# Last 64 keys of two head pairs: float32 64x64 products behind the product with v, in place of split half-row products

## The chip, the cores and the metric

One core of one Trainium2 chip runs the whole program. The metric is the device time of one execution in microseconds (us), the median of several runs.

## The reference

The program is an attention layer with sigmoid weights, followed by a mixture of eight experts. `q`, `k` and `v` have the shape (8 batches, 12 heads, 448 tokens, 64), in float32.

```python
scores = scale * np.matmul(q, k.transpose(0, 1, 3, 2)) - np.log(S)   # scale = 1/8, S = 448
attn = 1.0 / (1.0 + np.exp(-scores))
x = np.matmul(attn, v).astype(np.float32)      # then (B*S, H*D) = (3584, 768)
logits = x @ w_gate                            # 8 experts, 448 tokens each at most
# all (token, expert) pairs in falling order of logit; a pair is taken
# if its token is still free and its expert not full
out[mask_e] = np.maximum(x[mask_e] @ w1[e], 0.0) @ w2[e]
```

The weights are `w1` (8, 768, 1024) and `w2` (8, 1024, 768). The choice of experts hangs on the order of the logits, so the attention is computed to float32 accuracy.

## The kernel before

**Three parts.** The attention runs first, over 48 pairs of heads (8 batches of 6 pairs). Then the router finds each expert's tokens. Then the experts' two matrix products run, with the routing of later experts between them.

**A pair.** The two heads of a pair lie on the two halves of the 128 partitions: head j has partitions 64j to 64j+63, which are its 64 dimensions (`LO` and `HI` in the code). `load` brings k and q of a pair, and v of two pairs. `turn` (L394) transposes k and q of a pair on VectorE into `kqT` (L398), then `split` writes a high part `kqH` in float32r on ScalarE (L404) and the rest `kqL` on VectorE (L405). Keys times queries are then three products, high by high, high by low and low by high (`products`, L414 to L416). Each is one matrix instruction for each of the two heads, on rows 0 to 63 and on rows 64 to 127 of the array.

**Chunks of keys.** The 448 keys of a pair are three chunks of 128 and a rest of 64. `scores(b, pr, c)` computes chunk c for both heads into a tile `sc` of PSUM, of which there are three, and ScalarE's sigmoid (L428) writes the tile `at`. The rests of two neighbouring pairs, an even one and the odd one behind it, share one tile: `c == 3`, run with the odd pair. It first computes the last 128 keys of the even pair into all 128 rows, and then the last 64 keys of the odd pair over rows 0 to 63. What stays in rows 64 to 127 are the last 64 keys of the even pair.

**Product with v.** `av` (L441) multiplies the three full chunks by v, in plain float32. A float32 product in source is two matrix instructions in the trace. The two heads use the two halves of the array's columns. For an odd pair, four more float32 products take the rests of both pairs (L447). Each of them uses 64 rows and 64 columns of the array, and they go to two tiles `tp` of PSUM, of which there are two in all. VectorE then copies (L449) and adds (L451) into `xt`.

**Order.** The order in each engine is that of the program. Iteration i of the loop over pairs does: loads (on even pairs), `turn` of pair i+1, chunk 0 of the scores of pair i, `split` of pair i+1, the other chunks of pair i, up to two pieces of background work, and then `av` of pair i-1. Background work is the gate's logits of a finished batch (L462, added into `LE` at L464) and, for the first batch, the transposes of its rows (L473) with copies on VectorE (L478). Those of the other batches come after the loop, with copies on ScalarE (L476). Tiles `kqT`, `kqH` and `kqL` have two buffers each, which pairs take in turn.

Of the kernel before, what the change touches and what calls it, by code (L numbers as in the profile page):

```python
# [7 lines left out]
F32 = mybir.dt.float32  # L8
# [5 lines left out]
AF = mybir.ActivationFunctionType  # L14
# [11 lines left out]
AT_BUFS = 8  # L26
# [16 lines left out]
def _s32(v):  # L43
    v &= 0xFFFFFFFF
    return v - (1 << 32) if v >= (1 << 31) else v
# [65 lines left out]
class Router:  # L111
# [42 lines left out]
    def search(self, pe):  # L154
# [7 lines left out]
        nc.vector.tensor_copy(KE, p[:, :224])  # L162
        T, JP = K.c0, None
        X = None if pe else self.bank().bitcast(I32)
        for st in range(16):
            sh = 30 - 2 * st
            cnt = wk.tile([128, 3], BF, name="r_cnt") if pe else K.CN
            for i in range(3):
                junk = wk.tile([128, 224], BF, name="r_junk")
                nc.vector.tensor_scalar(junk, KE, T[:, i:i + 1].bitcast(F32), None, OP.is_ge, OP.add,  # L170
                                        accum_out=cnt[:, i:i + 1])
# [24 lines left out]
            if st == 0:  # L196
# [4 lines left out]
                nc.vector.tensor_scalar(nJ, PF, _s32(0x80000000), J, OP.bitwise_or, OP.bitwise_xor)  # L201
                T = wk.tile([128, 3], I32, name="r_T")
                nc.vector.tensor_scalar(T, K.kk[:, 1], nJ, None, OP.bitwise_xor)
            else:
                if st < 15:
                    T = wk.tile([128, 3], I32, name="r_T")
                    nc.vector.scalar_tensor_tensor(T, acc.bitcast(I32).to_broadcast([128, 3]), sh, nX,
                                                   OP.logical_shift_left, OP.bitwise_xor)
# [123 lines left out]
def moe_attention(tc, q, k, v, w_gate, w1, w2, out):  # L332
    nc = tc.nc
    B, H, S, D = q.shape
# [5 lines left out]
    with contextlib.ExitStack() as ctx:  # L340
# [7 lines left out]
        ps_s = pctx.enter_context(tc.tile_pool(name="pa_s", bufs=3, space=PSUM))  # L348
        ld = actx.enter_context(tc.tile_pool(name="ld", bufs=2))
        wk = actx.enter_context(tc.tile_pool(name="wk", bufs=2))  # L350
# [5 lines left out]
        bias = cp.tile([128, 1], F32, name="bias")  # L356
# [4 lines left out]
        LO, HI = slice(0, 64), slice(64, 128)  # L361
        def load(b, g, qq=nc.gpsimd, vq=nc.sync):


            nat["v", b, g] = ld.tile([128, G4, 3, D], F32, name="nv", bufs=3)
            nat["r", b, g] = ld.tile([128, 2, D], F32, name="nr", bufs=3)
            for i in range(2):
                t = nat["kq", b, 2 * g + i] = ld.tile([128, 2, S // 32, 32], F32, name="nkq", bufs=4)
                for n, (qn, src) in enumerate(((nc.sync, k), (qq, q))):
                    for j in range(2):  # L370
                        rws = src[b, g * G4 + 2 * i + j].rearrange("(c p) (x d) -> x p c d", p=32, x=2)
                        for x in range(2):
                            o = 64 * j + 32 * x
                            qn.dma_start(t[o:o + 32, n], rws[x])  # L374
            vs = v[b, g * G4:(g + 1) * G4]
            for h in range(G4):
                vq.dma_start(nat["v", b, g][:, h], vs[h, :384].rearrange("(c p) d -> p c d", p=128))
            for i in range(2):
                vq.dma_start(nat["r", b, g][HI if i == 0 else LO],
                             vs[2 * i:2 * i + 2, 384:].rearrange("h p d -> p h d"))  # L380
# [9 lines left out]
        for s in range(4):  # L390
            nc.sync.dma_start(wgz[:, :, s, 8 * s:8 * s + 8], w_gate.rearrange("(c p) e -> p c e", p=128))

        KQ = {}
        def turn(b, pr):  # L394


            T = wk.tile([128, 2, S], F32, name="kqT")
            nc.vector.transpose(T.rearrange("p n t -> p (n t)"), nat["kq", b, pr].rearrange("p n c d -> p (n c d)"))  # L398
            H = wk.tile([128, 2, S], F32R, name="kqH")
            L = wk.tile([128, 2, S], F32R, name="kqL")  # L400
            KQ[b, pr] = [x[:, i] for i in range(2) for x in (H, L)]

            def split():
                nc.scalar.activation(H, T, AF.Copy)  # L404
                nc.vector.tensor_tensor(L, T, H.bitcast(F32), OP.subtract)  # L405
            return split

        AT = {}

        def products(p, b, pr, keys, m):  # L410


            KH, KL, QH, QL = KQ[b, pr]
            for i, (R, M) in enumerate(((KH, QH), (KH, QL), (KL, QH))):  # L414
                for j, half in enumerate((LO, HI)):
                    nc.tensor.matmul(p[:m, j, :S], R[half, keys], M[half], start=i == 0, stop=i == 2)  # L416

        def scores(b, pr, c):


            a = AT[b, pr, c] = wk.tile([128, 2, S], F32, name="at", bufs=AT_BUFS)
            p = ps_s.tile([128, 2, 512], F32, name="sc")
            if c < 3:
                products(p, b, pr, slice(c * 128, c * 128 + 128), 128)
            else:
                products(p, b, pr - 1, slice(S - 128, S), 128)
                products(p, b, pr, slice(S - 64, S), 64)
            nc.scalar.activation(a, p[:, :, :S], AF.Sigmoid, bias=bias, scale=1 / math.sqrt(D))  # L428

        XT = {}  # L430

        def av(b, pr):


            if pr == 0:
                XT[b] = xa.tile([128, NP, S], F32, name="xt", bufs=XT_BUFS)
            p = ps_t.tile([128, 512], F32, name="tp")
            g, h0 = (2 * pr) // G4, (2 * pr) % G4
            for c in range(3):
                for j in range(2):  # L440
                    nc.tensor.matmul(p[j * 64:j * 64 + 64, :S], nat["v", b, g][:, h0 + j, c, :],  # L441
                                     AT[b, pr, c][:, j, :], start=(c == 0), stop=(c == 2 and pr % 2 == 0))
            if pr % 2:
                r = ps_t.tile([128, 512], F32, name="tp")
                for j in range(2):
                    for half, o in ((HI, r), (LO, p)):
                        nc.tensor.matmul(o[j * 64:j * 64 + 64, :S], nat["r", b, g][half, j, :],  # L447
                                         AT[b, pr, 3][half, j, :], start=o is r, stop=True)
            nc.vector.tensor_copy(XT[b][:, pr, :], p[:, :S])  # L449
            if pr % 2:  # L450
                nc.vector.tensor_tensor(XT[b][:, pr - 1, :], r[:, :S], XT[b][:, pr - 1, :], OP.add)  # L451
# [4 lines left out]
        def logits(b, prs):  # L456

            s, g = b % 4, b // 4
            p = ps_t.tile([128, 512], F32, name="tp")
            for pr in prs:  # L460
                for c in range(NCH):
                    nc.tensor.matmul(p[32 * c:32 * c + 32, :CP], wgz[:, pr, s, :], XT[b][:, pr, c * CP:(c + 1) * CP],  # L462
                                     start=(pr == prs[0]), stop=(pr == prs[-1]))
            nc.vector.tensor_tensor(LE[:, g], LE[:, g], p[:, :CP], OP.add)  # L464
# [17 lines left out]
        pairs = [(b, pr) for b in range(B) for pr in range(NP)]  # L482
        NPR = len(pairs)
        turn(*pairs[0])()
        bg, late = [], []
        for i in range(NPR + 1):
            cur = pairs[i] if i < NPR else None
            nxt = pairs[i + 1] if i + 1 < NPR else None
            old = pairs[i - 1] if i else None
            if cur and cur[1] % 2 == 0:  # L490
                nx = i // 2 + 2
                if nx < NPR // 2:
                    load(nx // 3, nx % 3)
            split = turn(*nxt) if nxt else None
            for c in range(4 if cur and cur[1] % 2 else 3 if cur else 0):
                scores(*cur, c)
                if c == 0 and split:
                    split()
            for _ in range(2):
                if bg:  # L500
                    bg.pop(0)()
            if old:
                av(*old)
            if i == 2:
                route_consts(nc, cp, K)
            if old == (B - 1, NP - 2):
                bg.append(lambda: logits(B - 1, range(NP - 2)))
            if old and old[1] == NP - 1:
                b = old[0]
                if b < B - 1:  # L510
                    bg.append(lambda b=b: logits(b, range(NP)))
                for c in range(NCH):
                    for hf in range(2):
                        if b >= B - LATE:
                            late.append(lambda b=b, c=c, hf=hf: rows(b, c, hf, "act"))
                        else:
                            bg.append(lambda b=b, c=c, hf=hf: rows(b, c, hf, "dve"))
# [8 lines left out]
        ps_s = ctx.enter_context(tc.tile_pool(name="ps_s", bufs=2, space=PSUM))  # L526
        ps_a = ctx.enter_context(tc.tile_pool(name="ps_a", bufs=2, space=PSUM))
        R = Router(tc, K, cp, rw, ps_a)
# [208 lines left out]
        for kx in range(E):  # L737
            turned = kx + 1 == E
            start = clock[0]
# [16 lines left out]
            for step, cost in enumerate(moe(kx)):  # L756
# [9 lines left out]
                if t >= t_chore:  # L766
                    c = next((c for c in chores if c[0] <= t), None)
# [37 lines left out]
```

## Time and profile before

| what | before |
|---|---|
| median of 3 runs | 913.71 us (912.76 to 914.37) |
| profiled execution | 915.77 us, its span 914.0 us |
| TensorE matrix instructions | 860.7 us busy, 94% of the span |
| VectorE | 535.1 us, 59% |
| ScalarE | 457.7 us, 50% |
| GpSimd | 463.7 us, 51% |
| attention | from 0 to about 303 us of the span |
| router alone, with the late rows | about 303 to 356 us |
| experts | about 356 to 914 us |

All times of rows below are from the one profiled execution, in us from the start of its span. A row of the timeline has the start, the duration from the first start to the last end, the engine, the line, the operation, the tile written and the tiles read, the part of the array (rows\*columns), the shape that is streamed, the count, and in brackets the idle time of the engine before it and what ended it. PE is TensorE's matrix engine and PEld its loading of the stationary operand; DVE is VectorE, ACT is ScalarE. The end of a matrix instruction is modelled, and neighbours overlap, so distances between starts tell more than durations.

### The profile page before, as it was taken

What the parts mean: (1) busy time and instruction counts of PE and PEld (TensorE: products, weight loads), DVE (VectorE), ACT (ScalarE), POOL (GpSimd) and SP (SyncE); (2) the same over time, 40 slices, a digit from 0 to 9 for tenths busy, and PEclk for the clock granted to TensorE, in tenths of its full rate; (3) what the DMA queues carried; (4) which work ended last, traced back from release to release, by engine and by line L of the source; (5) the groups of instructions that cost most, each with busy time, mean ns of one, the idle gap of its engine ahead of it and who ended that gap; (6) DMA issues with size and microseconds to landing.
All of it is one profiled execution on the core that took longest, in us unless ns stands there. A gap on an engine that the chain in (4) does not pass through costs nothing.

```text
span 914.0 us, 16457 instructions
## 1 busy us (share of the span) xinstructions
PE 860.7 (94%) x5603; PEld 656.2 (72%) x5603; DVE 535.1 (59%) x2053; ACT 457.7 (50%) x633; POOL 463.7 (51%) x442
## 2 busy tenths in 40 slices
PE   5898999999999774998999999999999999999997
PEld 3444555555555444987998888988988888989996
DVE  3645455555554588876968969959779632330110
ACT  5565676676677472443433534534434434544441
POOL 8533444444430003573675675684784783741651
PEclk9999999999999996999899999999999999999999
DMA  9646665555550486324434343353452442632421
GB/s 176 140 97 149 126 128 117 116 125 118 116 121 1 127 277 185 108 82 149 140 114 146 122 147 124 128 151 113 154 162 96 141 154 90 213 117 82 158 76 61
DMA packets 205236, 117.59 MB, mean 129 GB/s; under 512 B 145728, under 2 KB 194880, under 8 KB 205152
## 3 DMA queue, kind: packets, MB, share of 16 engines
q1 hardware_dynamic: 190688, 83.03, 35.2%
q0 software_dynamic: 10752, 33.05, 11.4%
q10 hardware_dynamic: 3712, 0.46, 0.3%
q8 instruction: 44, 0.72, 0.3%
q14 instruction: 40, 0.33, 0.1%
HBM read 94.47 MB, written 22.02 MB: 127 GB/s over the span
## 4 chain that ended last, share of the span: by engine, by line
PE 78%; DVE 11%; issue 4%; DMA 2%; POOL 2%; ACT 2%; SPq 0%; POOLq 0%; ACTq 0%; DVEq 0%
PE sc L416 14%; PE tp L441 12%; PE sc L671 9%; PE sc L669 9%; PE sc L673 9%; PE sc L706 6%; PE sc L708 6%; PE sc L704 6%; DVE r_junk L170 3%; PE tp L447 2%; PE tp L634 2%; PE tp L621 2%; DMA xr<-xs,r_idx 1%; PE tp L462 1%; POOL wl L587 1%
## 5 line engine op out<-in xcount | busy, mean ns | idle before, releaser
L587 POOL TENSOR_TENSOR wl<-wr,wh 128x768 fp32r<-128x768 f32 (+1 forms) x96 | 205.7, 2151 | 135.5 <-ACT wh L585 124.6
L428 ACT ACTIVATE at<-sc,bias 128x896 f32<-128x896 f32 x168 | 160.6, 1003 | 63.2 <-PE sc L416 62.9
L374 POOL DMA_DIRECT2D nkq<-in_q_dram x184 | 115.5, 640 | 142.3 <-DVE kqT L398 132.9
L708 PE MATMUL sc<-hh,wl 128*128 128x448 f32 (+2 forms) x400 | 151.4, 379 | 0.0
L673 PE MATMUL sc<-xh,wl 128*128 128x448 f32 (+2 forms) x396 | 146.7, 370 | 0.0
L671 PE MATMUL sc<-xl,wh 128*128 128x448 f32 (+2 forms) x396 | 146.3, 370 | 0.0
L706 PE MATMUL sc<-hl,wh 128*128 128x448 f32 (+2 forms) x400 | 145.5, 364 | 0.2 <-POOL hl L681 0.2
L669 PE MATMUL sc<-xh,wh 128*128 128x448 f32 (+2 forms) x396 | 145.4, 367 | 0.0
L704 PE MATMUL sc<-hh,wh 128*128 128x448 f32 (+2 forms) x400 | 143.9, 360 | 0.0
L170 DVE TENSOR_SCALAR_CACHE_REDUCE r_junk<-r_KE,r_T 128x224 bf16<-128x224 f32 x315 | 123.3, 442 | 0.1
L441 PE MATMUL tp<-at,nv 128*64 128x448 f32 x576 | 118.8, 548 | 4.8 <-DVE xr L478 4.4
L585 ACT ACTIVATE wh<-wr 128x768 fp32r<-128x768 f32 (+1 forms) x112 | 102.0, 939 | 9.7 <-DMA wr<-in_moe_w_dram 9.7
L405 DVE TENSOR_TENSOR kqL<-kqT,kqH 128x896 fp32r<-128x896 f32 x48 | 52.4, 1092 | 68.5 <-ACT kqH L404 68.5
L681 POOL TENSOR_TENSOR hl<-yt,hh 128x896 fp32r<-128x896 f32 x32 | 68.2, 2132 | 46.7 <-ACT yt L680 45.1
L416 PE MATMUL sc<-kqH 64*128 64x448 f32 (+1 forms) x384 | 79.3, 410 | 11.7 <-ACT kqH L404 8.8
L677 ACT ACTIVATE hh<-sc 128x896 fp32r<-128x896 f32 x32 | 29.4, 919 | 111.5 <-PE sc L673 111.5
L441 PEld LDWEIGHTS tp<-at,nv 128*64 128x64 f32 x576 | 37.0, 136 | 63.7 <-issue 55.3
L706 PEld LDWEIGHTS sc<-hl,wh 128*128 128x128 f32 x400 | 75.2, 188 | 7.3 <-issue 1.1
L671 PEld LDWEIGHTS sc<-xl,wh 128*128 128x128 f32 x396 | 75.5, 191 | 6.5 <-issue 0.4
L669 PEld LDWEIGHTS sc<-xh,wh 128*128 128x128 f32 x396 | 75.7, 191 | 5.7
L607 POOL DMA_INDIRECT xr<-xs,r_idx x32 | 31.9, 997 | 94.0 <-ACT wh L585 83.2
L673 PEld LDWEIGHTS sc<-xh,wl 128*128 128x128 f32 x396 | 75.5, 191 | 5.0
(155 smaller groups left out, 1327.3 us busy)
## 6 DMA issues: line engine op xcount, KB each, us to landing
wr<-in_moe_w_dram SPq DMA_DIRECT2D x64, 384.0 KB, 3.0
wr<-in_moe_w_dram SPq DMA_DIRECT2D x48, 512.0 KB, 3.9
nkq<-in_k_dram SPq DMA_DIRECT2D x192, 56.0 KB, 2.5
xs<-xr SPq DMA_DIRECT2D x32, 336.0 KB, 3.3
nkq<-in_q_dram POOLq DMA_DIRECT2D x184, 56.0 KB, 2.6
nv<-in_v_dram SPq DMA_DIRECT2D x92, 96.0 KB, 2.4
nr<-in_v_dram SPq DMA_DIRECT2D x46, 32.0 KB, 2.3
xr<-xs,r_idx POOLq DMA_INDIRECT x32, 4.6
```

What stands on the lines that cost most here:

```text
L170: nc.vector.tensor_scalar(junk, KE, T[:, i:i + 1].bitcast(F32), None, OP.is_ge, OP.add, accum_out=cnt[:, i:i + 1])
L374: qn.dma_start(t[o:o + 32, n], rws[x])
L416: nc.tensor.matmul(p[:m, j, :S], R[half, keys], M[half], start=i == 0, stop=i == 2)
L428: nc.scalar.activation(a, p[:, :, :S], AF.Sigmoid, bias=bias, scale=1 / math.sqrt(D))
L441: nc.tensor.matmul(p[j * 64:j * 64 + 64, :S], nat["v", b, g][:, h0 + j, c, :], AT[b, pr, c][:, j, :], start=(c == 0), stop=(c == 2 and pr ...
L587: eng.tensor_tensor(lo, raw[u], hi.bitcast(F32), OP.subtract)
L669: nc.tensor.matmul(ph[:, f, lo:hi], wh[:, a, fs], xh[:, dd, lo:hi], start=st, stop=False)
L671: nc.tensor.matmul(ph[:, f, lo:hi], wh[:, a, fs], xl[:, dd, lo:hi], start=False, stop=False)
L673: nc.tensor.matmul(ph[:, f, lo:hi], wl[:, a, fs], xh[:, dd, lo:hi], start=False, stop=en)
L704: nc.tensor.matmul(py[:, d2, :w], wh[:, a, dsl], h1, start=st, stop=False)
L706: nc.tensor.matmul(py[:, d2, :w], wh[:, a, dsl], h2, start=False, stop=False)
L708: nc.tensor.matmul(py[:, d2, :w], wl[:, a, dsl], h1, start=False, stop=(j == 1 and a == 3))
```

## The change

The rest's scores are no longer made of split operands, and no longer with the odd pair's chunks. A new `rest_scores` makes them from `kqT` itself, in float32: for each of the two pairs and each of the two heads one product of the last 64 keys, on 64 rows and 64 columns of the array. The even pair's keys go to rows 64 to 127 of the tile, the odd pair's to rows 0 to 63, as before. It is called on iterations of even pairs, right behind `av` of the odd pair before, for the current (even) and the next (odd) pair. `kqT` gets three buffers, since it is now read by the matrix engine an iteration later. `scores` does three chunks for every pair; `products` is folded into it.

```diff
-            T = wk.tile([128, 2, S], F32, name="kqT")
+            T = KT[b, pr] = wk.tile([128, 2, S], F32, name="kqT", bufs=3)
...
         def scores(b, pr, c):
             a = AT[b, pr, c] = wk.tile([128, 2, S], F32, name="at", bufs=AT_BUFS)
             p = ps_s.tile([128, 2, 512], F32, name="sc")
-            if c < 3:
-                products(p, b, pr, slice(c * 128, c * 128 + 128), 128)
-            else:
-                products(p, b, pr - 1, slice(S - 128, S), 128)
-                products(p, b, pr, slice(S - 64, S), 64)
-            nc.scalar.activation(a, p[:, :, :S], AF.Sigmoid, bias=bias, scale=1 / math.sqrt(D))
+            KH, KL, QH, QL = KQ[b, pr]
+            for i, (R, M) in enumerate(((KH, QH), (KH, QL), (KL, QH))):
+                for j, half in enumerate((LO, HI)):
+                    nc.tensor.matmul(p[:, j, :S], R[half, c * 128:(c + 1) * 128], M[half], start=i == 0, stop=i == 2)
+            sigmoid(a, p)
+
+        def rest_scores(b, pr):
+            a = AT[b, pr, 3] = wk.tile([128, 2, S], F32, name="at", bufs=AT_BUFS)
+            p = ps_s.tile([128, 2, 512], F32, name="sc")
+            for o, T in ((HI, KT[b, pr - 1]), (LO, KT[b, pr])):
+                for j, half in enumerate((LO, HI)):
+                    nc.tensor.matmul(p[o, j, :S], T[half, 0, S - 64:S], T[half, 1], start=True, stop=True)
+            sigmoid(a, p)
...
-            for c in range(4 if cur and cur[1] % 2 else 3 if cur else 0):
+            for c in range(3 if cur else 0):
                 scores(*cur, c)
...
             if old:
                 av(*old)
+            if cur and cur[1] % 2 == 0:
+                rest_scores(*nxt)
```

## Rows read from the trace of the kernel before

**Rows 1.** The page: busy time by engine, and the chain's shares by engine.

```profile
PE 860.7 (94%) x5603; PEld 656.2 (72%) x5603; DVE 535.1 (59%) x2053; ACT 457.7 (50%) x633; POOL 463.7 (51%) x442
...
PE 78%; DVE 11%; issue 4%; DMA 2%; POOL 2%; ACT 2%; SPq 0%; POOLq 0%; ACTq 0%; DVEq 0%
```

**Rows 2.** Busy time in stretches: length, engines (instructions), granted clock, DMA share, GB/s.

```profile
107.83:242.00 134.17, 134.17 (x1120) 72.17 (x1116) 70.11 (x85) 96.09 (x104) 57.64 (x92) 1.00 0.60 122
...
303.00:345.00 42.00, 29.70 (x213) 18.76 (x205) 34.79 (x196) 25.71 (x56) 0.00 (x0) 1.00 0.72 231
```

**Rows 3.** Waits of the matrix engine, 0 to 300 us: total, times, longest.

```profile
PE sc L416 <- ACT kqH L404: 8.8, 1, 8.8
PE tp L441 <- DVE xr L478: 4.4, 3, 1.6
PE sc L416 <- ACT at L428: 2.9, 1, 2.9
```

**Rows 4.** Timeline of the matrix engine, one even and one odd pair.

```profile
241.98 0.47 PE L416 MATMUL sc<-kqH 64*128 64x448 f32 x2
...
243.70 0.37 PE L416 MATMUL sc<-kqH,kqL 64*128 64x448 f32 x2
244.00 2.48 PE L441 MATMUL tp<-at,nv 128*64 128x448 f32 x12
246.40 0.98 PE L447 MATMUL tp<-at,nr 64*64 64x448 f32 x8
247.32 0.47 PE L416 MATMUL sc<-kqH 64*128 64x448 f32 x2
...
249.06 0.37 PE L416 MATMUL sc<-kqH,kqL 64*128 64x448 f32 x2
249.36 0.47 PE L416 MATMUL sc<-kqH 64*128 64x448 f32 x2
...
249.87 0.37 PE L416 MATMUL sc<-kqH,kqL 64*128 64x448 f32 x2
250.07 0.36 PE L416 MATMUL sc<-kqH 64*64 64x448 f32 x2
...
250.77 2.48 PE L441 MATMUL tp<-at,nv 128*64 128x448 f32 x12
253.17 0.47 PE L416 MATMUL sc<-kqH 64*128 64x448 f32 x2
```

**Rows 5.** Timeline, matrix engine alone, 247.02 to 247.3: second half of L447's eight.

```profile
246.83 0.56 PE L447 MATMUL tp<-at,nr 64*64 64x448 f32 x4
```

**Rows 6.** Timeline of the weight loads within one product with v.

```profile
244.43 0.14 PEld L441 LDWEIGHTS tp<-at,nv 128*64 128x64 f32 x2 [0.23 <-issue]
244.80 0.14 PEld L441 LDWEIGHTS tp<-at,nv 128*64 128x64 f32 x2 [0.23 <-issue]
```

**Rows 7.** One line's instructions: duration min/median/max, first and last start, forms.

```profile
L447 PE MATMUL tp<-at,nr x192: 536/562/587, 24.2 to 303.0; 64*64 64x448 f32 x192
```

**Rows 8.** Timeline of ScalarE, the odd pair of rows 4.

```profile
248.29 1.01 ACT L428 ACTIVATE at<-sc,bias 128x896 f32<-128x896 f32 x1 [1.70 <-PE sc L416]
250.33 0.95 ACT L404 ACTIVATE kqH<-kqT 128x896 fp32r<-128x896 f32 x1 [1.02 <-PE sc L416]
251.18 2.79 ACT L428 ACTIVATE at<-sc,bias 128x896 f32<-128x896 f32 x3
```

**Rows 9.** Timeline of VectorE, the same odd pair.

```profile
251.31 1.09 DVE L405 TENSOR_TENSOR kqL<-kqT,kqH 128x896 fp32r<-128x896 f32 x1 [1.68 <-ACT kqH L404]
```

**Rows 10.** Timeline of all engines, an odd pair with row copies on VectorE.

```profile
70.86 0.95 ACT L404 ACTIVATE kqH<-kqT 128x896 fp32r<-128x896 f32 x1 [1.01 <-PE sc L416]
...
72.85 1.01 DVE L478 COPY xr<-tp 112x384 f32<-112x384 f32 x2
73.46 2.48 PE L441 MATMUL tp<-at,nv 128*64 128x448 f32 x12 [1.28 <-DVE xr L478]
```

**Rows 11.** Timeline of the matrix engine at the one long stall of the loop.

```profile
33.98 0.64 PE L416 MATMUL sc<-kqH 64*128 64x448 f32 x2 [2.92 <-ACT at L428]
...
37.54 0.97 PE L441 MATMUL tp<-at,nv 128*64 128x448 f32 x4
```

More of the change, by code (lines that the diff above doesn't have):

```diff
@@ L391, in moe_attention @@
             nc.sync.dma_start(wgz[:, :, s, 8 * s:8 * s + 8], w_gate.rearrange("(c p) e -> p c e", p=128))
-        KQ = {}
+        KQ, KT = {}, {}
         def turn(b, pr):
-            T = wk.tile([128, 2, S], F32, name="kqT")
+            T = KT[b, pr] = wk.tile([128, 2, S], F32, name="kqT", bufs=3)
             nc.vector.transpose(T.rearrange("p n t -> p (n t)"), nat["kq", b, pr].rearrange("p n c d -> p (n c d)"))
@@ L408, in moe_attention, with sigmoid, scores @@
         AT = {}
-        def products(p, b, pr, keys, m):
+        def sigmoid(a, p):
+            nc.scalar.activation(a, p[:, :, :S], AF.Sigmoid, bias=bias, scale=1 / math.sqrt(D))
+        def scores(b, pr, c):
+            a = AT[b, pr, c] = wk.tile([128, 2, S], F32, name="at", bufs=AT_BUFS)
+            p = ps_s.tile([128, 2, 512], F32, name="sc")
             KH, KL, QH, QL = KQ[b, pr]
@@ L415, in products @@
                 for j, half in enumerate((LO, HI)):
-                    nc.tensor.matmul(p[:m, j, :S], R[half, keys], M[half], start=i == 0, stop=i == 2)
-        def scores(b, pr, c):
-            a = AT[b, pr, c] = wk.tile([128, 2, S], F32, name="at", bufs=AT_BUFS)
+                    nc.tensor.matmul(p[:, j, :S], R[half, c * 128:(c + 1) * 128], M[half], start=i == 0, stop=i == 2)
+            sigmoid(a, p)
+        def rest_scores(b, pr):
+            a = AT[b, pr, 3] = wk.tile([128, 2, S], F32, name="at", bufs=AT_BUFS)
             p = ps_s.tile([128, 2, 512], F32, name="sc")
-            if c < 3:
-                products(p, b, pr, slice(c * 128, c * 128 + 128), 128)
-            else:
-                products(p, b, pr - 1, slice(S - 128, S), 128)
-                products(p, b, pr, slice(S - 64, S), 64)
-            nc.scalar.activation(a, p[:, :, :S], AF.Sigmoid, bias=bias, scale=1 / math.sqrt(D))
+            for o, T in ((HI, KT[b, pr - 1]), (LO, KT[b, pr])):
+                for j, half in enumerate((LO, HI)):
+                    nc.tensor.matmul(p[o, j, :S], T[half, 0, S - 64:S], T[half, 1], start=True, stop=True)
+            sigmoid(a, p)
         XT = {}
```

## The prediction

> **What bounds the kernel now.** I read the page first: the matrix engine is busy 94% of the span and holds 78% of the chain that ended last [rows 1]. A share over the whole span says nothing of the stage that is touched, so next come the stretches: between 107.83 and 242.00 us, in the middle of the attention, the matrix engine is busy 134.17 us of 134.17, at full granted clock, while ScalarE has 96.09 us, VectorE 70.11 us and DMA a share of 0.60 [rows 2]. The view of waits says the same from the other side: in the whole loop it waits for 8.8 us at the start and some 7 us in four other places, and no DMA stands among its releasers after the start [rows 3]. So in the attention the end is set by the distance between one matrix instruction's start and the next, and that is what the timeline shows: an even and an odd pair repeat every 253.17 - 241.98 = 11.19 us [rows 4]. What is taken from this sequence ends the attention earlier, and the router behind it starts with the last pair's sums, so it moves with it.
>
> **What goes.** The scores of an even pair, three chunks, take 244.00 - 241.98 = 2.02 us from their first start to the first start of the product with v. Those of an odd pair, with the rest as a fourth chunk, take 250.77 - 247.32 = 3.45 us [rows 4]. Without the rest an odd pair's block is an even one's, so 3.45 - 2.02 = 1.43 us go for each two pairs. Inside it are six pairs of instructions at about 0.20 us and 0.2 us for a late start (0.30 from 249.06 to 249.36, where neighbours stand 0.20 apart, and a slow first step behind it).
>
> **What comes.** Four float32 products of 64 rows by 64 columns with 448 streamed columns are eight instructions in the trace, in just the form of L447: 64\*64 64x448 f32 [rows 7]. L447's eight start as four within 0.03 us at 246.40 and four at 246.83 [rows 4, 5]; the next work starts at 247.32. Within the product with v one step of two plain float32 instructions takes 244.80 - 244.43 = 0.37 us [rows 6]. Eight more behind L447's eight are two more steps of four on the same part of the array. The lower bound is 2 x 0.37 = 0.75 us, where nothing drains between; the upper one is L447's whole stay, 247.32 - 246.40 = 0.92 us. I take 0.75, since the weights of a step can be loaded during the step before, as rows 6 show for the product with v.
>
> In the even and odd pair together that is 1.43 - 0.75 = 0.68 us less (0.51 by the upper bound). L447 has 192 instructions, eight at a time: 24 times [rows 7]. 24 x 0.68 = 16.3 us (12.2).
>
> Here a rule speaks. A change from 64\*128 to 128\*64 costs 0.10 us in the rows: 0.30 from 243.70 to 244.00, where neighbours stand 0.20 apart; but 64\*64 follows 64\*128 at 250.07 just 0.20 behind 249.87 [rows 4], so that change is free. The Trainium skill, TensorEngine Tiling (Array Packing), Tiling Modes (Key Properties), says that changing the tiling mode drains the engine. The trace bears this out for the first change and not for the second. By the rule the new instructions still cost no drain, as they follow L447 in its own mode; anywhere else in the loop they would add two, and 24 x 2 x 0.10 = 4.8 us of the gain would go.
>
> **The sigmoid that moves.** The number of sigmoids stays; the rest's comes now before the odd pair's first one. Three waits must be followed, with T the start of the odd pair's first chunk.
> - The rest's last step starts 0.49 before T (as 246.83 before 247.32) and ends, with 0.56, at T + 0.07. ScalarE starts about 0.1 behind the end of a chunk's matrix work (chunk 0 of the odd pair starts at 247.32, its last pair ends near 248.19, the sigmoid starts at 248.29 [rows 8]) and takes 1.0, so it is through at T + 1.17. The odd pair's third chunk takes the same PSUM tile (three in turn). Its first weights are wanted at T + 1.13 and its first product at T + 1.33; the release takes some 0.06 (248.29 + 1.01 = 249.30 to 249.36). So it may be late by between 0 and 0.1 us; I take 0.05, 24 x 0.05 = 1.2 us back (bounds 0 and 2.4).
> - `kqH` of the next pair was held back: it waited 1.02 us for the rest's first products, which read the buffer that it overwrites, and came at 250.33, T + 3.01 [rows 8]. That wait goes. It now stands behind the sigmoids of the rest and of chunk 0, at T + 2.2, ends at 3.1, and `kqL` (1.09 us [rows 9]) at 4.2. The next even pair starts at T + 2.02 + 2.40 = T + 4.42 and wants `kqL` at 4.73. It is in time by 0.5 us.
> - ScalarE has seven sigmoids of 1.0 and two copies of 0.95 in two pairs, 8.9 us of a period of then 10.5. It stays beside the path.
>
> `kqT` in three buffers costs nothing: the third is free an iteration before VectorE wants it, and nobody else waits for it. Nothing is moved past a load: GpSimd's and SP's queues keep their order, and the loads of k, q and v come two groups ahead. The same bytes in 6% less time bring a DMA share of 0.60 to 0.64.
>
> **Two places where it differs.** While the first batch's rows are copied on VectorE, the product with v waits for those copies, 1.28 us at 73.46, and these stand behind `kqL`, which waits for `kqH` at 70.86 [rows 10]. There the odd pair's block ends not with the matrix engine but with that chain, which comes 3.01 - 2.2 = 0.8 us earlier, against 1.43. That loses 0.6, and 0.3 in the odd pair two earlier (logits and their add in the same place): 0.9 us back. Even pairs keep their wait. At the stall of 2.92 us at 33.98 us the matrix engine waits for a sigmoid behind a late `kqH`, and its nine pairs of instructions then run 3.56 us to 37.54 instead of 2.02 [rows 11]. The changed order gives that tile back one sigmoid earlier, and a shorter stall may leave the clock up; I take 0.8 us gained (0 to 2).
>
> **The sum.** -16.3 + 1.2 + 0.9 - 0.8 = -15.0 us. The profiled execution, 915.77 us, would become 900.8. Its own time lies 2.06 above the median of the runs, 913.71; the difference is carried over to that median: 898.7 us. The router and the experts are untouched; their clock changes at stalls and the router stretch of 42 us with 29.70 of matrix work [rows 2] can fall a little differently, which I give 2 us either way.
>
> **Rivals.**
> 1. *Part of it comes back as waits at the sigmoid.* If the new instructions stay for 0.92 us, their sigmoid ends so much later, and the third chunk waits 0.2 us in full: 1.43 - 0.92 - 0.2 = 0.31, 24 x 0.31 = 7.4 us, 906.3 us. For it: the margin above is nearly zero. Against it: the form is L447's to the letter.
> 2. *Slower: the quarters don't run beside each other.* The new products of the two heads write two banks of one tile, and both pairs' products for a head write one bank; L447's go to two tiles. If for this, or for the shared streamed operand, only two ran at a time, the stay would be four steps of 0.37 = 1.5 us against 1.43 that go: +1.7 us, 915.4; one at a time, eight steps, 3.0 us: +37 us, 951. The point from which it decides is 1.43 us of stay. Against it: rows 4 and 5 show four starts at once, and L447 also streams distinct parts of few tiles. The Trainium skill, FP8 and Floating Point Precision, TensorE Precision Notes, counts four passes for true float32, one more than the three split products; by the passes alone, two instructions at a time as the split ones run, the new form would be the slower one, near the first of these two times. No row here shows plain float32 slower than L447's steps.
> 3. *It changes nothing.* The loop gets shorter but the router's or the experts' stalls grow by as much, at a weight load or a gather that comes no earlier. For it: DMA share of 0.72 in the router's stretch [rows 2]. Against it: all of these are issued by work that moves along. 913.5 us.
>
> **Chances.** The forecast has 0.73, with its own range 895.5 to 902.5 (bounds of the step, the sigmoid's wait and the clock). Rival 1 has 0.18, rival 2 0.05, rival 3 0.04. A measurement of this kernel can tell about 0.2% from no change. Faster: 0.92, the forecast, rival 1 and a little of rival 3; same: 0.04; slower: 0.04. The range of 8 in 10 takes the forecast's and most of rival 1: 894.8 to 904.8.
>
> **What would show it.** Right: the attention ends near 288 us instead of 303; two pairs repeat every 10.5 us; a block of L447 and the new line starts next work 1.67 us behind its first start; odd blocks of L416 last 2.0 us; `kqH` waits no longer for the matrix engine on odd pairs. Wrong: the new eight start two by two, or a gap stands before the third chunk of odd pairs with a sigmoid as releaser (rival 1), or the loop ends at 288 and the span does not follow (rival 3). A stay of the new instructions of over 1.43 us would turn the sign.

## The result

The changed kernel takes 903.83 us (median of 4, 897.91 to 905.92) against 914.04 us for the kernel before (median of 4 beside it): ratio 0.988, 95% interval 0.983 to 0.993. Run again beside other kernels it took 903.23 us (6 runs) against 914.60 (22 runs): 0.987, interval 0.985 to 0.990. That is 10.2 and 11.4 us less where 15.0 were forecast. The time lies inside the range, near its upper end, and outside the forecast's own range (895.5 to 902.5).

**The steady part.** First the matrix engine's timeline of an even and an odd pair, the counterpart of [rows 4 and 5]. L421 is the split scores, L445 the product with v, L451 its rests, L431 the new float32 products. Lines that stand at `...` are left out.

```profile
244.36 0.47 PE L421 MATMUL sc<-kqH 64*128 64x448 f32 x2
...
246.38 2.48 PE L445 MATMUL tp<-at,nv 128*64 128x448 f32 x12
248.79 0.98 PE L451 MATMUL tp<-at,nr 64*64 64x448 f32 x8
249.59 0.93 PE L431 MATMUL sc<-kqT 64*64 64x448 f32 x8
250.45 0.47 PE L421 MATMUL sc<-kqH 64*128 64x448 f32 x2
...
251.57 0.37 PE L421 MATMUL sc<-kqH,kqL 64*128 64x448 f32 x2
251.78 0.43 PE L421 MATMUL sc<-kqH 64*128 64x448 f32 x2
252.04 0.36 PE L421 MATMUL sc<-kqL,kqH 64*128 64x448 f32 x2
...
252.54 2.48 PE L445 MATMUL tp<-at,nv 128*64 128x448 f32 x12
254.95 0.47 PE L421 MATMUL sc<-kqH 64*128 64x448 f32 x2
```

Two pairs repeat every 254.95 - 244.36 = 10.59 us, where it was 11.19. From L451's first start to the next split scores are 250.45 - 248.79 = 1.66 us (forecast 1.67), where it was 0.92: the new products stay for 0.74. The odd pair's scores take 252.54 - 250.45 = 2.09 us instead of 3.45, and 0.07 of them is the late third chunk: its second step stands 0.27 behind its first (251.78 to 252.04), where neighbours stand 0.20 apart. The weight loads name the releaser, and ScalarE's timeline (the counterpart of [rows 8]) says why:

```profile
251.73 0.19 PEld L421 LDWEIGHTS sc<-kqH 64*128 64x128 f32 x2 [0.17 <-ACT at L411]
```

```profile
250.67 1.91 ACT L411 ACTIVATE at<-sc,bias 128x896 f32<-128x896 f32 x2 [1.71 <-PE sc L431]
252.47 0.95 ACT L404 ACTIVATE kqH<-kqT 128x896 fp32r<-128x896 f32 x1
```

The rests' sigmoid starts 0.22 us behind T = 250.45 (forecast 0.17), and gives its PSUM tile back 0.05 later than worked out. `kqH` comes at T + 2.02 and waits for nothing (it came at T + 3.01).

**The first 90 us.** Here the larger part of the missing gain was lost. In the waits of the matrix engine up to 300 us, against [rows 3], the stall at the start and the waits for row copies on VectorE are still there:

```profile
PE sc L421 <- ACT kqH L404: 11.3, 2, 8.7
PE tp L445 <- DVE xr L482: 4.8, 3, 1.7
```

The first line holds the start (8.7) and the stall at 32 us (2.6). And the loop shows a second stretch at half the clock, which the profile of before did not have. Stretches of the changed kernel (columns as in rows 2), and the product with v that falls into the second of them:

```profile
68.20:71.60 3.40, 1.75 (x16) 1.18 (x16) 1.96 (x4) 3.40 (x4) 2.51 (x4) 1.00 0.65 173
71.60:75.00 3.40, 3.40 (x10) 1.05 (x11) 0.28 (x1) 0.02 (x1) 0.00 (x0) 0.50 0.79 188
```

```profile
71.47 4.17 PE L445 MATMUL tp<-at,nv 128*64 128x448 f32 x12 [1.65 <-DVE xr L482]
75.57 0.47 PE L421 MATMUL sc<-kqH 64*128 64x448 f32 x2
```

The engine was busy 1.75 us of 3.40, waited 1.65 for a row copy, and then ran at 1.2 GHz, the lower level: 75.57 - 71.47 = 4.10 us for a product with v that takes 2.41. At the stall itself, the counterpart of [rows 11], it starts 1.86 us earlier (32.12 against 33.98), but it then waits 0.66 us more, for `kqL`, which is ready only 1.0 us earlier than before. And the stretch at half clock, 34.1 to 37.5 us in either kernel, now covers a product with v as well:

```profile
32.12 0.47 PE L421 MATMUL sc<-kqH 64*128 64x448 f32 x2 [2.61 <-ACT kqH L404]
33.24 0.47 PE L421 MATMUL sc<-kqL,kqH 64*128 64x448 f32 x2 [0.66 <-DVE kqL L405]
...
35.88 3.25 PE L445 MATMUL tp<-at,nv 128*64 128x448 f32 x12
39.05 0.61 PE L451 MATMUL tp<-at,nr 64*64 64x448 f32 x4
```

That stretch, before and after:

```profile
34.10:37.50 3.40, 3.40 (x18) 2.58 (x18) 1.62 (x4) 3.40 (x5) 2.22 (x5) 0.50 0.80 142
```

```profile
34.10:37.50 3.40, 3.40 (x18) 1.72 (x16) 1.73 (x2) 3.40 (x4) 2.15 (x4) 0.50 0.75 146
```

**The account.** The last rests of the product with v start at 303.0 us before [rows 7] and 291.8 us after, 11.2 us earlier. Up to the start of the 13th pair (89.98 us before, 89.06 after) there are only 0.9 us of it; from there to the 47th (288.04 and 277.43) 9.7 us in 17 times two pairs, 0.57 each; the end brings 0.6. The first starts of the two pairs, before and then after, and L451's summary line of after:

```profile
89.98 0.48 PE L416 MATMUL sc<-kqH 64*128 64x448 f32 x2
...
288.04 0.47 PE L416 MATMUL sc<-kqH 64*128 64x448 f32 x2
```

```profile
89.06 0.47 PE L421 MATMUL sc<-kqH 64*128 64x448 f32 x2
...
277.43 0.47 PE L421 MATMUL sc<-kqH 64*128 64x448 f32 x2
```

```profile
L451 PE MATMUL tp<-at,nr x192: 536/562/587, 23.3 to 291.8; 64*64 64x448 f32 x192
```

In the router some 0.4 of the 11.2 us are lost again. At the second expert 1.5 come back, where a stretch at half clock lasts 3.4 us instead of 6.8, and 0.6 at 801.6 us, where a wait of 0.45 us for VectorE is gone. So the span falls by 12.8 us, from 914.0 to 901.2.

### The profile page after: what moved, and what is told of

Same layout as the page of the kernel before. It is cut to its first block, busy times and chain, and to the rows that moved or that the text cites. A ratio compares the mean times of both kernels' runs of the same rounds, so it can differ in the third digit from the quotient of the medians.

```text
span 901.2 us, 16245 instructions
## 1 busy us (share of the span) xinstructions
PE 848.1 (94%) x5507; PEld 640.1 (71%) x5507; DVE 535.4 (59%) x2053; ACT 456.4 (51%) x633; POOL 464.5 (52%) x442
## 4 chain that ended last, share of the span: by engine, by line
PE 75%; DVE 11%; issue 6%; POOL 4%; DMA 2%; ACT 2%; SPq 0%; POOLq 0%; ACTq 0%; DVEq 0%
PE tp L445 13%; PE sc L421 10%; PE sc L677 8%; PE sc L675 8%; PE sc L679 8%; PE sc L712 6%; PE sc L714 6%; PE sc L710 6%; DVE r_junk L170 3%; PE tp L451 2%; PE sc L431 2%; PE tp L640 2%; PE tp L627 2%; POOL wl L593 2%; POOL hl L687 1%
## 5 line engine op out<-in xcount | busy, mean ns | idle before, releaser
L445 PE MATMUL tp<-at,nv 128*64 128x448 f32 x576 | 121.3, 557 | 5.2 <-DVE xr L482 4.8
L445 PEld LDWEIGHTS tp<-at,nv 128*64 128x64 f32 x576 | 37.7, 138 | 64.9 <-issue 56.2
L593 DVE TENSOR_TENSOR wl<-wr,wh 128x768 fp32r<-128x768 f32 (+1 forms) x16 | 25.1, 1572 | 91.6 <-ACT wh L591 79.3
```

What stands on the lines that cost most here:

```text
L593: eng.tensor_tensor(lo, raw[u], hi.bitcast(F32), OP.subtract)
```

## The experiments

Theory A: the loop is set by the distances between the matrix engine's starts, the change is worth 0.6 us for each two pairs, and some 2.5 us of that were lost in the first 90 us to stalls and the clock behind them. Rival B: the sigmoid's wait eats the gain. Rival C: the new place and the freed `kqH` bring it, not the form. Rival D: the change is worth no more than what was measured.

**The rests twice.** The four products are issued a second time into the same tile.

```diff
-            for o, T in ((HI, KT[b, pr - 1]), (LO, KT[b, pr])):
-                for j, half in enumerate((LO, HI)):
-                    nc.tensor.matmul(p[o, j, :S], ...)
+            for _ in range(2):
+                for o, T in ((HI, KT[b, pr - 1]), (LO, KT[b, pr])):
+                    for j, half in enumerate((LO, HI)):
+                        nc.tensor.matmul(p[o, j, :S], ...)
```

> The changed kernel with the four float32 products of the rests issued twice over, into the same PSUM tile (the second time gives the same values), so that their price is measured in place. Theory A (the loop is set by the distances between the matrix engine's starts; the eight new instructions cost 0.74 us behind L447's eight, all on the path): eight more cost two more steps of 0.37 us, 24 x 0.74 = 17.8 us more than the changed kernel, near 921 us; two pairs repeat every 11.33 us instead of 10.59. Rival B (the price is mostly waits for the sigmoid of the rests, and matrix time is partly hidden by them): under 10 us more, and the gap before the odd pair's third chunk changes.

919.37 us (7 runs), 15.5 above the changed kernel's 903.83. Matrix engine:

```profile
119.64 0.98 PE L452 MATMUL tp<-at,nr 64*64 64x448 f32 x8
120.45 1.68 PE L432 MATMUL sc<-kqT 64*64 64x448 f32 x16
122.06 0.47 PE L421 MATMUL sc<-kqH 64*128 64x448 f32 x2
```

Sixteen stay 1.61 us where eight stay 0.86: 0.75 for eight more, two steps of 0.37. The price is matrix time and wholly on the path: 24 x 0.75 = 18. Its loop ends at 307.5 us, 17.9 us behind that of the changed kernel's second profile (289.6, below), which like this one has no fall of the clock among the row copies. B falls as the main cause.

**The rests ahead of the product with v.**

```diff
+            if cur and cur[1] % 2 == 0:
+                rest_scores(*nxt)
             for _ in range(2):
                 if bg:
                     bg.pop(0)()
             if old:
                 av(*old)
-            if cur and cur[1] % 2 == 0:
-                rest_scores(*nxt)
```

> The changed kernel with the rests' products ahead of the product with v of the pair before (and of the background work), instead of behind it. Theory A: the stay is the same two steps of 0.37 us; the late third chunk of odd pairs (0.07 us each, 0.35 in three of 24) goes, since the sigmoid of the rests runs during the product with v, and the rests may wait up to 0.2 us for chunk 0's PSUM tile: between 3 us faster and 3 us slower than the changed kernel, near it. By the drain rule of the Trainium skill, TensorEngine Tiling (Array Packing), Tiling Modes (Key Properties), a change of mode more for each two pairs: about 0.1 us x 24 = 2.4 us slower. Rival B (the third chunk's wait is what eats the gain): faster by 24 x 0.07 to 24 x 0.35, 2 to 8 us.

903.37 us (4 runs), no different from the changed kernel. Matrix engine, an even pair:

```profile
123.20 0.37 PE L421 MATMUL sc<-kqH,kqL 64*128 64x448 f32 x2
123.50 0.98 PE L431 MATMUL sc<-kqT 64*64 64x448 f32 x8
124.41 2.48 PE L445 MATMUL tp<-at,nv 128*64 128x448 f32 x12
126.82 0.98 PE L451 MATMUL tp<-at,nr 64*64 64x448 f32 x8
127.73 0.47 PE L421 MATMUL sc<-kqH 64*128 64x448 f32 x2
```

Apart, the two groups of eight stay 0.91 each, 1.82 us; joined, 1.66. So standing behind the product's rests saves 0.16 us, and the late third chunk, which is in time when the rests stand ahead, takes 0.07 of that back. The Trainium skill, TensorEngine Tiling (Array Packing), Tiling Modes (Key Properties), says that a change of mode drains the engine; the trace agrees in so far as one more change of mode for each two pairs goes with 0.16 us here (0.10 expected). The place is worth 0.09 us, 2 us in all, which the runs don't resolve.

**The place alone.** The rests stay split, in six half-row pairs as before, but stand where the change puts them.

```diff
-            for o, T in ((HI, KT[b, pr - 1]), (LO, KT[b, pr])):
-                for j, half in enumerate((LO, HI)):
-                    nc.tensor.matmul(p[o, j, :S], T[half, 0, S - 64:S], T[half, 1], start=True, stop=True)
+            for n, (KH, KL, QH, QL) in ((128, KQ[b, pr - 1]), (64, KQ[b, pr])):
+                for i, (R, M) in enumerate(((KH, QH), (KH, QL), (KL, QH))):
+                    for j, half in enumerate((LO, HI)):
+                        nc.tensor.matmul(p[:n, j, :S], R[half, S - n:S], M[half], start=i == 0, stop=i == 2)
```

> The place alone: the rests stay split and in six half-row pairs of instructions as in the kernel before, but stand behind the product with v of the odd pair before, as in the changed kernel. Theory A: six steps of 0.20 us stay, 1.2 us against 0.74 us of the float32 form, so 24 x 0.46 = 11 us slower than the changed kernel, and about 24 x 0.2 = 5 us faster than the kernel before for the late start that goes: near 909 to 914 us. Rival C (the place, which frees kqH earlier and takes the tile's wait away, brings the gain, and the form little): near the changed kernel, 900 to 905 us.

914.83 us (10 runs) against 914.63: ratio 1.0004 (0.9992 to 1.0017). Matrix engine:

```profile
118.21 0.98 PE L452 MATMUL tp<-at,nr 64*64 64x448 f32 x8
119.13 0.47 PE L432 MATMUL sc<-kqH 64*128 64x448 f32 x2
...
120.45 0.37 PE L421 MATMUL sc<-kqH 64*128 64x448 f32 x2
```

The six pairs stay 1.32 us, and L452's rests in front of them 0.92, as L447's did before. The 5 us that I expected for the late start did not come: of the 0.2 us half is back as a slow first step at the new place, and the third chunk behind it is late (121.48 to 121.78 us in its timeline, 0.30). C falls: without the form the place is worth nothing, though it too frees `kqH` early.

**The third buffer for `kqH` alone, in the kernel before.**

```diff
-            H = wk.tile([128, 2, S], F32R, name="kqH")
+            H = wk.tile([128, 2, S], F32R, name="kqH", bufs=3)
```

> The kernel before with a third buffer for kqH and nothing else, so that kqH of the next pair no longer waits 1.02 us for the rests' first products. Theory A (in the steady part the matrix engine's starts set the end, and kqH is in time in either kernel): two pairs still repeat every 11.19 us; only the odd pairs with row copies on VectorE end earlier (about 0.8 us, twice): within 2 us of the kernel before. Rival C (the freed kqH is a part of the gain): two pairs repeat faster, 3 us or more in all.

915.13 us (10 runs) against 914.60: ratio 1.0006 (0.9989 to 1.0023). ScalarE, and the starts of two odd pairs on the matrix engine:

```profile
121.81 0.95 ACT L404 ACTIVATE kqH<-kqT 128x896 fp32r<-128x896 f32 x1 [0.36 <-DVE kqT L398]
```

```profile
119.46 0.47 PE L416 MATMUL sc<-kqH 64*128 64x448 f32 x2
...
130.65 0.47 PE L416 MATMUL sc<-kqH 64*128 64x448 f32 x2
```

`kqH` no longer waits for the matrix engine (1.02 us before), and two pairs still repeat every 11.19 us. The wait that went was not on the path.

**One piece of background work per pair, in both kernels.** The first batch's row transposes then take one of the two PSUM tiles at a time.

```diff
-            for _ in range(2):
+            for _ in range(1):
                 if bg:
                     bg.pop(0)()
```

> The changed kernel with one piece of background work per pair instead of two, so that the product with v finds a free PSUM tile while the first batch's rows are copied. Theory A (about 4 us of the steady gain is lost at two stalls of the matrix engine in the first 90 us, by the waits for row copies, 4.8 us in all, and by the clock at 0.5 from 71.6 to 75.0 us): the waits go and the clock stays up there; 5 to 7 us faster than the changed kernel, 897 us, and the runs lie closer together. Rival B (the shortfall lies in the steady part): no change in the steady part and less than 2 us in all.

> The kernel before with one piece of background work per pair instead of two, the partner of the changed kernel with the same edit (896.43 us). Theory A (the change is worth 0.60 us for each two pairs, 24 times, and what the first 90 us took from it are stalls and the clock that came down there): without those stalls the difference of the two is near the full 14.4 us; this kernel gains the waits for row copies, 4.7 us, and comes to 909 to 911 us. Rival D (the change itself is worth only the 10 us measured, and the edit helps the changed kernel more by chance): this kernel near 906 us.

The changed kernel falls to 896.43 us (4 runs), ratio 0.980 (0.978 to 0.983) to the kernel before; the kernel before falls to 911.28 (11 runs), 0.995 (0.993 to 0.997). Waits of the matrix engine in the loop, the changed kernel first:

```profile
PE sc L421 <- ACT kqH L404: 11.2, 2, 8.7
PE sc L421 <- DVE kqL L405: 1.0, 2, 0.6
```

```profile
PE sc L416 <- ACT kqH L404: 8.7, 1, 8.7
PE sc L416 <- ACT at L428: 2.9, 1, 2.9
PE sc L416 <- DVE kqL L405: 1.0, 2, 0.7
```

The waits for row copies are gone from both, and between them lie 911.28 - 896.43 = 14.85 us. In the loops of the two profiles it is 298.1 - 283.6 = 14.5, by the last starts of the rests, the changed kernel first:

```profile
L451 PE MATMUL tp<-at,nr x192: 536/562/587, 23.6 to 283.6; 64*64 64x448 f32 x192
```

```profile
L447 PE MATMUL tp<-at,nr x192: 536/562/587, 24.1 to 298.1; 64*64 64x448 f32 x192
```

So without the waits for row copies the change is worth more than the 10.2 and 11.4 measured, and D falls. Not all of the 14.5 is the steady part: the profile of the changed kernel has no stretch at half clock at 34 us, that of the other has one, and its nine pairs of instructions there take 3.40 us (33.86 to 37.26) instead of 2.02. Without these 1.4 us some 13.1 are left, near 24 x 0.57 = 13.7. How often either kernel has that stretch, one profile of each does not show.

**VectorE's constants spread.** In addition to one piece, the VectorE instructions for the router's constants (25 in the code and in the trace, not 27) run two to a pair, not all behind the third pair. `route_consts` now returns them as a list; that part of the edit is left out here.

```diff
+            for _ in range(2):
+                if consts:
+                    consts.pop(0)()
             if i == 2:
-                route_consts(nc, cp, K)
+                consts = route_consts(nc, cp, K)
```

> The changed kernel with one piece of background work per pair, and with VectorE's 27 instructions for the router's constants spread, two to a pair from the fourth pair on, instead of all at once behind the third. Theory A: the stall of 2.7 us near 30 us goes, in which the matrix engine waits for a late transpose of k and q, and with it the clock's fall behind it in those executions that have one: 2.5 to 4.5 us less than with one piece alone, 892 to 894 us. If the stall came from the loads and not from VectorE's constants, it stays and the time is 896 us.

891.75 us (5 runs, 890.57 to 892.10), ratio 0.974 (0.972 to 0.977): the best version of this study, 4.7 us less than with one piece alone. The stall near 30 us is gone. So it came from the constants: VectorE in the changed kernel worked on them from 25.4 to 30.0 us, and the transpose of k and q stood behind them:

```profile
28.87 1.14 DVE L103 TENSOR_SCALAR c_kk<-c_t 128x3 int32<-128x3 int32 x15
29.92 1.10 DVE L398 STREAM_TRANSPOSE kqT<-nkq 128x896 f32<-128x896 f32 x1
```

The loop has no stretch at half clock, but that of one piece alone had none either, although it kept the stall; so whether the stall brings the clock down each time is not shown. The loops of the two profiles differ by 2.7 us (283.6 and 280.9); of the rest, some 1.6 go with a shorter stretch at half clock at the second expert, 3.4 us instead of 6.8. Matrix engine:

```profile
27.88 2.48 PE L447 MATMUL tp<-at,nv 128*64 128x448 f32 x12
30.29 0.47 PE L423 MATMUL sc<-kqH 64*128 64x448 f32 x2
...
32.30 2.48 PE L447 MATMUL tp<-at,nv 128*64 128x448 f32 x12
```

**The changed kernel again.**

> The changed kernel once more, beside the others on the same chip, for its spread and its clock. Theory A: its times lie further apart than those of the kernel before (897.9 to 905.9 against 912.8 to 914.6) since stalls in the first 90 us bring the clock down in some executions and not in others: each profile shows none to two stretches of 3.4 us at the lower level there, and a profile with one less is about 2 us shorter in the loop.

903.23 us (6 runs, 900.20 to 904.87). Its profile has the fall of the clock at 34 us, but none among the row copies, after the same wait:

```profile
71.24 2.48 PE L445 MATMUL tp<-at,nv 128*64 128x448 f32 x12 [1.64 <-DVE xr L482]
73.65 0.47 PE L421 MATMUL sc<-kqH 64*128 64x448 f32 x2
```

2.41 us instead of 4.10, and the loop ends at 289.6 us instead of 291.8: 1.7 of these 2.2 us are the fall. It comes in one execution and not in the next. That the change makes the times lie further apart is not borne out: the kernel before ranged from 912.65 to 918.71 beside it.

## Why the prediction was right, and where its size was off

- *What bounds the kernel*: right. Doubling the new products cost their full matrix time; taking the wait of `kqH` away cost and gained nothing.
- *What goes, what comes*: right. 1.43 us less and 0.74 more (forecast 0.75); four starts at once, as L447's. Rival 2 did not occur.
- *The sigmoid that moves*: right in place, low in size. The third chunk is 0.07 us late 20 times of 23 (0.05 forecast) and 0.35 to 0.39 three times, where ScalarE starts the rests' sigmoid late (240.08 us for matrix work that ended near 239.66); together some 2.5 us against 1.2. The three are the 8th, 24th and 40th pair, and the same ones are late in the profiles of the changed kernel's second run and of its two versions with one piece; so the delay belongs to the program and is no chance, but what delays ScalarE there was not tried. This is rival 1 in kind, at the bound that the forecast gave, not at its price of 0.31 us left per two pairs: 0.57 to 0.60 are left.
- *Two places where it differs*: here the size failed. The odd pairs among the row copies lost 0.4 us each against the steady ones (their blocks went from 5.62 and 5.60 us to 4.63 and 4.61), 0.8 in all, as forecast (0.9). But the term for the stall, 0.8 us gained, was wrong in sign: the engine started earlier, then waited 0.66 us for `kqL` and ran a product with v at half clock, 0.8 us longer than its 2.41 (35.88 to 39.05). The two pairs around the stall take 15.77 us (24.95 to 40.72 us) where they took 15.72 (25.14 to 40.86), so their steady gain of 0.6 is gone too. The forecast had a sigmoid's order set this stall; the constants on VectorE set it, which the change does not touch. And a fall of the clock after the wait for a row copy, 1.7 us, had no term in the sum. The forecast put the clock's 2 us either way on the router and the experts; in this profile 1.5 came back at the second expert.
- *Sum*: the loop came out 11.2 us shorter instead of 15.0: 1.4 for the steady part (24 x 0.57 = 13.7 against 24 x 0.63 = 15.1) and some 2.4 for the first 90 us. With the row copies out of the way, kernel against kernel, the medians differ by 14.85, where the forecast's sum without its 0.9 for the row copies is 15.9.
- *Where luck comes in*: 903.83 lies nearer to rival 1's 906.3 than to the forecast's 898.7, and inside the range because that took in most of rival 1's. It is the rows, 0.74 us of stay and 0.57 to 0.60 left for each two pairs, that decide for the forecast's mechanism; the number alone does not.

## What to carry to other kernels

Where one engine's starts follow each other without a gap, count its steps: here a product that uses a quarter of the array, four at a time, beat three split products on half of it, although float32 takes twice the instructions per product. A group on the array's small tiles was cheapest right behind another of the same tiling, by 0.16 us. When a shorter loop gives less than its steps promise, look first at the few stalls outside the steady part, what waits in them and what the clock does behind them: two small edits there brought the changed kernel from 903.2 to 891.8 us, as much as the change itself.

## What the runs showed that was not expected

The same wait of 1.65 us brought the granted clock to 0.5 in one execution and not in another of the same kernel; what decides it was not tried. Eight plain float32 instructions of 64\*64 stay 0.91 us alone and 0.75 behind eight of the same tiling, so a change of tiling goes with 0.16 us there, while a change from 64\*128 to 64\*64 in the kernel before cost nothing that its row shows [rows 4]. With the rests ahead that change does show: L431 starts 0.30 us behind the last split pair (123.20 to 123.50), where neighbours stand 0.20 apart. Whether the form of the products or the tiling makes the difference is not shown.
